# Parking buffers held for good, product banks that swap roles, and earlier splits in the last block

## The chip, the cores and the metric

The kernel runs on one core of one Trainium2 chip. The metric is the device time of one execution in microseconds (us). All tensors are float32, the weights among them arrive as 64-bit floats.

## What is computed

The reference is a chain of three parts: attention within chunks of 64 positions, then two feed-forward layers over 4608 tokens.

```python
scores = (1/8) * q_c @ k_c.T          # 8 batches x 8 heads, chunks of 64, head size 64
attn = softmax(scores); x = (attn @ v_c) -> 4608 x 512
h = x @ w_in          # 512 x 2048
g = max(h, 0) + alpha * min(h, 0)
x = g @ w_out         # 2048 x 512
h = x @ w_in2;  g = h - tanh(h);  out = g @ w_out2
```

(In the code the two layers' weights are moe_w_in, moe_w_out and moe2_w_in, moe2_w_out, or views of them.)

## The kernel before, in words

**Numbers.** TensorE works on pairs: every float32 operand is split into a high part (a rounding copy to fp32r, made by ScalarE) and a low part (operand minus high part, made by VectorE or GpSimd), and each product is three matmuls: high by high, low by high, high by low. Each 64-bit weight block is turned into float32 by two ScalarE instructions (lines 115 and 118) and four VectorE instructions (lines 128, 132, 134, 138), from a raw tile "rw".

**Stages on TensorE.** The tokens are nine blocks of 512. The first two blocks of layer one run in `step_first` and the beginning of the main loop. `step_one` then does layer one for one block by one 128-wide slice of the hidden width per step: 12 matmuls up (line 539), 12 down (line 609, which need the pair "ghi", "glo"), while a table of events (`at(step, fn, place=...)`, fired by `fire` at five places of a step) puts the attention of later blocks, the loads and the weight work between them. From about 742 us on, `two_blocks` runs pairs of blocks with a seven-product scheme (products p1 to p7 of 2x2 blocks, six matmuls each): five passes s = 0 to 4 of eight `cycle(s, p)`, where s = 0 finishes layer one and s = 1 to 4 do layer two; then eight `small(p)` for the last block, and a tail. In a cycle the products go into four banks X, Y (names "hpb") and H0, H1 ("hps"); between them `downs(n)` issues n down matmuls (line 1091) of units in a line, and `split_ahead(n)` makes the pairs of the first n units of that line: "ghi" on ScalarE (line 567), "glo" on GpSimd (line 570). `c11`, `c12`, `c22`, `c21` are the gates that read the finished banks: a few ScalarE instructions (`square`, `second`, `edge`) and VectorE instructions (`drain`, `close`; lines 587, 588, 598 to 600). Line 1190 is the VectorE sum of two banks (`add`), line 1193 the ScalarE copy of a bank.

**Parking.** The seven-product scheme needs sums of weight blocks. They are made in advance and stored ("parked") in device memory. A parking has four functions: `park_load` (DMA of the raw weights into "rw"), `park_form` (conversion and sums), `park_split` (high and low part), `park_store`. There are 16 units of kind "u" (layer two's up weights), each with a unit "u1" (layer one's up weights, which come from pairs already on chip) that goes along with it, one unit in four steps from step 36 on; then 16 of kind "d" (layer two's down weights): six in the last steps of the loop, ten in `two_blocks`, set out there by `when` every 11.5 us of an assumed time. Sums and low parts are made on GpSimd (lines 217, 225, 247), high parts on ScalarE (line 246). Tiles "rw", "mw" and "whi" come from one rotating pool tag with two buffers, "mr" from another with one.

**Order.** The instructions of each engine stay in the order in which the code issues them. All DMAs go through one queue engine, SyncE (SP), in order; a DMA that has to wait for its data holds back those behind it. The queue also carries the loads of queries and keys (line 332), 16 each in a burst, and the fetches of parked weights (line 274).

Of the kernel before, what the change touches and what calls it, by code (L numbers as in the profile page):

```python
# [9 lines left out]
F32 = mybir.dt.float32  # L10
F32R = mybir.dt.float32r
I32 = mybir.dt.int32
U32 = mybir.dt.uint32
I64 = mybir.dt.int64
# [13 lines left out]
def kernel(  # L28
# [19 lines left out]
    nc = tc.nc  # L48
# [3 lines left out]
    P = 128  # L52
# [141 lines left out]
    wu, wd2, parked = {}, {}, {}  # L194

    def park_load(kind, n, c):
        raw = wide.tile([P, 512], I64, tag="w", name="rw")
        if kind == "d":
            load_raw(raw, 1, n, 1)
        else:  # L200
            nc.sync.dma_start(
                out=raw.rearrange("p (g m) -> p g m", g=2),
                in_=w_in2[:, n * 2 * P:(n + 1) * 2 * P].rearrange("(g c p) m -> p g c m", p=P, c=2)[:, :, c, :],
            )
        parked[kind, n, c] = raw

    def park_form(kind, n, c):

        if kind == "u1":
            mr = wide.tile([P, 8, P], F32, tag="w", name="mw")  # L210
# [8 lines left out]
        else:  # L219
            mr = wide.tile([P, 8, P], F32, tag="r", name="mr", bufs=1)  # L220
# [7 lines left out]
    def park_split(kind, n, c):  # L228

        mr = parked[kind, n, c]  # L230
        hi = mr.bitcast(F32R) if kind == "u1" else wide.tile([P, 8, P], F32R, tag="w", name="whi")
# [14 lines left out]
        nc.scalar.activation(out=h, in_=m, func=AF.Copy)  # L246
# [541 lines left out]
    for j in range(2):  # L788
        at(KF + HF * (j + 1) - 1, load_half, j)
    for i in range(KF):  # L790
        n, c, step = i // 2, i % 2, 2 * KF + 4 + 4 * i
        at(step, park_load, "u", n, c)
        at(step, park_form, "u1", n, c)
        at(step + 1, park_split, "u1", n, c)
        at(step + 1, park_form, "u", n, c)
        at(step + 2, park_store, "u1", n, c, place=4)
        at(step + 2, park_split, "u", n, c)
        at(step + 3, park_store, "u", n, c, place=4)
    DP = 6
    for f in range(DP):  # L800
        step = 6 * KF + 4 + 2 * f
        at(step, park_load, "d", f, 0)
        at(step + 1, park_form, "d", f, 0, place=2)
        at(step + 1, park_split, "d", f, 0, place=4)
        at(step + 2, park_store, "d", f, 0, place=1)
# [297 lines left out]
    def split_ahead(n):  # L1103
        for u in line[:n]:
            u.split()
# [36 lines left out]
    def two_blocks(queue):  # L1142
# [6 lines left out]
        H0, H1 = (ps_h.tile([P, NB], F32, tag="h", name="hps") for _ in range(2))  # L1149
        p5 = ptb.rearrange("p e h a i -> p (e h a i)")  # L1150
# [62 lines left out]
        def on(s, p, place, fn, *args):  # L1213
            hooks.setdefault((s, p, place), []).append((fn, args))
# [62 lines left out]
        PLACES = {"start": 0.0, "p1": 1.4, "p5": 2.7, "p6": 4.1, "p2": 5.4, "p3": 6.8, "p7": 8.2, "p4": 12.2, "end": 14.2}  # L1277

        def when(us, fn, *args):
            p, us = divmod(us, 15.0)  # L1280
            place = max((x for x in PLACES if PLACES[x] <= us), key=PLACES.get)
            on(int(p) // NPAIR, int(p) % NPAIR, place, fn, *args)

        todo = []
        for i, f in enumerate(range(DP, KF)):
            todo += [(11.5 * i, park_load, f), (11.5 * i + 5.5, park_form, f), (11.5 * i + 8.5, park_split, f),
                     (11.5 * i + 11.4, park_store, f)]
        for us, fn, f in sorted(todo, key=lambda x: x[0]):
            when(us, fn, "d", f, 0)
        on(1, 0, "start", parks_done)  # L1290

        def cycle(s, p):
            turns = s > 0 and p % 4 == 0
# [65 lines left out]
        def small(p):  # L1359
# [13 lines left out]
            split_ahead(2)  # L1373
# [15 lines left out]
            split_ahead(2)  # L1389
            first.close()  # L1390
            downs(gaps[2])
            product(s, "p4", h1[:, :H], H)
            downs(gaps[3])
# [4 lines left out]
            split_ahead(2)  # L1398
# [61 lines left out]
```

## Time and profile before

| | |
|---|---|
| median of 3 runs | 1739.51 us (1736.46 to 1744.77) |
| the profiled execution | 1742.13 us, span 1740.4 us |
| TensorE matmuls (PE) | 1638.2 us busy, 94% of the span |
| VectorE (DVE) | 1233.6 us, 71% |
| ScalarE (ACT) | 994.7 us, 57% |
| GpSimd (POOL) | 447.5 us, 26% |
| mean granted TensorE clock | 0.975 of full speed |

The profile is of one execution; spans of an engine are its busy times. PE is the engine that is busy nearly all of the time, so the places where it is idle, and those where its clock is granted at less than full speed, are where time can come from. An entry such as "[3.10 <-DVE glo L570]" says that the instruction's engine was idle for 3.10 us before it and that the DVE instruction of line 570, which writes glo, released it.

### The profile page before, as it was taken

Reading aid. Unit: us, or ns where it says so; the run is one execution under the profiler, and the core shown is the slowest. Engines: PE = TensorE matmul, PEld = TensorE weight load, DVE = VectorE, ACT = ScalarE, POOL = GpSimd, SP = SyncE. Lnnn points to the kernel's source line nnn. Section 1 sums busy time; section 2 is a strip of 40 time slices with the busy share of each in tenths; the row PEclk is TensorE's granted clock in tenths of the full one; section 3 lists DMA queues with packets and bytes.
Section 4 is the critical chain, followed back from the end, with each engine's and each line's share of the span. In section 5 each row is a group of like instructions: output and inputs, shape, how many; then the busy total and the mean of one; then the engine's idle time right before and its main releaser. Section 6 shows DMA issues by size and latency. Waiting matters only on the chain.

```text
span 1740.4 us, 26381 instructions
## 1 busy us (share of the span) xinstructions
PE 1638.2 (94%) x9309; PEld 1339.0 (77%) x9309; DVE 1233.6 (71%) x1860; ACT 994.7 (57%) x1785; POOL 447.5 (26%) x406
## 2 busy tenths in 40 slices
PE   7899999989989999998889999999999999999988
PEld 7688887878768787776667877787777778787877
DVE  7878856767767786754367687768776877687763
ACT  5666534555545455554466566656766575656452
POOL 1000002343333342222142223222222232223223
PEclk9999999999999999998989999999999999999999
DMA  9551435556555575366657845554555355535540
GB/s 239 168 184 35 104 89 121 148 159 152 147 127 148 138 183 180 122 215 203 236 188 250 281 147 163 169 173 125 176 157 188 109 176 157 163 110 188 182 132 24
DMA packets 339299, 276.49 MB, mean 159 GB/s; under 512 B 180432, under 2 KB 244960, under 8 KB 339168
## 3 DMA queue, kind: packets, MB, share of 16 engines
q1 hardware_dynamic: 339168, 274.82, 53.4%
q8 instruction: 73, 1.20, 0.3%
q14 instruction: 58, 0.48, 0.1%
HBM read 192.95 MB, written 81.79 MB: 158 GB/s over the span
## 4 chain that ended last, share of the span: by engine, by line
PE 59%; DVE 12%; issue 10%; DMA 5%; ACT 5%; SPq 5%; POOL 4%; DVEq 0%; POOLq 0%; ACTq 0%
PE y L1091 19%; PE hpb L1183 13%; PE hps L539 10%; PE y L609 10%; PE hps L1183 5%; DMA rw<-in_moe_w_out_dram 3%; POOL glo L570 2%; SPq L332 2%; DMA wu<-whi 1%; SPq L298 1%; DVE mr L134 1%; DVE arena L587 1%; DVE mr L128 1%; DVE mr L138 1%; DVE glo L570 1%
## 5 line engine op out<-in xcount | busy, mean ns | idle before, releaser
L539 PE MATMUL hps<-x,w 128*128 128x512 f32 (+1 forms) x1356 | 336.0, 398 | 6.2 <-ACT kt L366 5.3
L570 POOL TENSOR_TENSOR glo<-arena,ghi 128x512 fp32r<-128x512 f32 x142 | 197.1, 1402 | 535.9 <-ACT ghi L567 384.7
L1183 PE MATMUL hpb<-w,wu 128*128 128x512 f32 (+1 forms) x1200 | 296.0, 391 | 28.0 <-DVE th L588 11.7
L539 PEld LDWEIGHTS hps<-x,w 128*128 128x128 f32 x1356 | 260.9, 194 | 62.8 <-ACT kt L366 5.8
L1091 PE MATMUL y<-w,ghi 128*128 128x512 f32 x1152 | 298.7, 392 | 9.7 <-ACT ghi L567 9.7
L1183 PEld LDWEIGHTS hpb<-w,wu 128*128 128x128 f32 x1200 | 226.6, 197 | 79.5 <-DVE th L588 14.2
L1091 PEld LDWEIGHTS y<-w,ghi 128*128 128x128 f32 x1152 | 214.9, 189 | 56.3 <-ACT ghi L567 13.5
L609 PE MATMUL y<-ghi,w 128*128 128x512 f32 x880 | 231.4, 395 | 4.2 <-ACT yst L634 3.5
L609 PEld LDWEIGHTS y<-ghi,w 128*128 128x128 f32 x880 | 161.7, 188 | 40.1 <-ACT yst L634 3.9
L1091 PE MATMUL y<-w,glo 128*128 128x512 f32 x576 | 164.7, 392 | 3.4 <-POOL glo L570 3.4
L1183 PE MATMUL hps<-w,wu 128*128 128x512 f32 (+1 forms) x624 | 138.9, 370 | 13.7 <-DVE hps L1190 13.7
L609 PE MATMUL y<-glo,w 128*128 128x512 f32 x440 | 129.7, 399 | 16.6 <-DVE glo L570 16.6
L1183 PEld LDWEIGHTS hps<-w,wu 128*128 128x128 f32 x624 | 111.0, 191 | 35.8 <-DVE hps L1190 15.4
L1091 PEld LDWEIGHTS y<-w,glo 128*128 128x128 f32 x576 | 108.3, 189 | 28.2 <-POOL glo L570 6.0
L567 ACT ACTIVATE ghi<-g 128x512 fp32r<-128x512 f32 x112 | 70.6, 630 | 95.3 <-DVE g L552 95.0
L552 DVE SCALAR_TENSOR_TENSOR g<-neg,nalpha_sb,g 128x512 f32<-128x512 f32 x112 | 91.8, 820 | 46.2 <-ACT g L551 46.2
L609 PEld LDWEIGHTS y<-glo,w 128*128 128x128 f32 x440 | 83.0, 190 | 37.3 <-DVE glo L570 20.3
L217 POOL TENSOR_TENSOR mw<-w 128x256 f32<-128x256 f32 x32 | 26.9, 860 | 313.8 <-DMA ysc<-yhalf 235.5
L591 ACT ACTIVATE w<-sq,bias_sb 128x512 f32<-128x512 f32 x144 | 104.2, 724 | 0.0
L594 ACT ACTIVATE ktc<-sq,edge_sb 128x512 f32<-128x512 f32 x144 | 103.9, 721 | 0.0
L1193 ACT ACTIVATE hps<-hpb 128x512 f32<-128x512 f32 x40 | 23.3, 582 | 134.4 <-PE hpb L1183 134.4
L599 DVE SCALAR_TENSOR_TENSOR arena<-sq,arena 128x512 f32<-128x512 f32 x116 | 97.0, 836 | 4.0
(171 smaller groups left out, 2562.0 us busy)
## 6 DMA issues: line engine op xcount, KB each, us to landing
wu<-wu SPq DMA_DIRECT2D x336, 256.0 KB, 3.2
g<-arena SPq DMA_DIRECT2D x67, 256.0 KB, 3.6
arena<-g SPq DMA_DIRECT2D x64, 256.0 KB, 3.7
raww<-in_moe_w_in_dram SPq DMA_DIRECT2D x16, 512.0 KB, 5.9
v<-in_v_dram SPq DMA_DIRECT2D x32, 256.0 KB, 3.9
raww<-in_moe_w_out_dram SPq DMA_DIRECT2D x16, 512.0 KB, 5.5
rw<-in_moe_w_in_dram SPq DMA_DIRECT2D x16, 512.0 KB, 5.3
wu<-mw SPq DMA_DIRECT2D x32, 256.0 KB, 3.3
```

The lines of the kernel that those rows point to most:

```text
L217: nc.gpsimd.tensor_tensor(out=quarters[:, :, e], in0=hi, in1=lo, op=ALU.add)
L332: nc.sync.dma_start(out=o, in_=i)
L539: nc.tensor.matmul(out=hp[:, cols], lhsT=w[:, a, m], rhs=x[b][:, kk, cols], start=(kk == 0 and i == 0), stop=(kk == KD - 1 and i == 2),)
L552: nc.vector.scalar_tensor_tensor(out=g, in0=neg, scalar=nalpha_sb[:, f:f + 1], in1=g, op0=ALU.mult, op1=ALU.add)
L567: nc.scalar.activation(out=hi, in_=g, func=AF.Copy)
L570: lo_engine.tensor_tensor(out=lo, in0=g, in1=hi.bitcast(F32), op=ALU.subtract)
L591: nc.scalar.activation(out=self.w, in_=self.sq, func=AF.Square, bias=bias_sb)
L594: nc.scalar.activation(out=self.mask, in_=self.sq, func=AF.Relu, bias=edge_sb)
L599: nc.vector.scalar_tensor_tensor(out=g, in0=self.sq, scalar=TS[0], in1=g, op0=ALU.add, op1=ALU.mult)
L609: nc.tensor.matmul(out=acc[t], lhsT=lhsT, rhs=rhs, start=(f == ends[0] and i == 0), stop=(f == ends[1] and i == 2))
L1091: nc.tensor.matmul(out=self.acc[t], lhsT=lhsT, rhs=rhs, start=(self.f == self.ends[0] and i == 0), stop=(self.f == self.ends[1] and i == 2),)
L1183: nc.tensor.matmul(out=o, lhsT=w[:, a, c], rhs=x[c][:, b, :h], start=start and i == 0 and c == 0, stop=i == 2 and c == 1, skip_group_check ...
```

## The change

- **Desk.** Three fixed tiles are made at step 36: `desk[0]` for raw loads, `desk[1]` for the u1 sums and for all high parts, `desk[2]` for the other sums. The steps of a unit are spread out: load at its first step, u1 sums and split two steps later, the u sums at the third, u split at the fourth, u store at the fifth step. The high part of a u1 unit is made on GpSimd and no longer on ScalarE. The d units are loaded one parking ahead; in `two_blocks` `when` and its times go, and each cycle has one d parking at fixed places (sums at p2, next load at p3, split at p4, store at the end), seven in s = 0 and three in s = 1.
- **Banks.** In odd cycles the pairs (X, Y) and (H0, H1) change places.
- **Last block.** `small` calls `split_ahead(3)` at its start and `split_ahead(2)` after p4, where it called `split_ahead(2)` at its start and after each gate's `drain`.

The line numbers of the kernel after the change are larger by 5 to 13 (park_load 206, park_form 222 and 230, park_split 252 to 255, ghi 575, products 1196, downs 1103).

```diff
--- before.py
+++ after.py
@@ -191,10 +191,15 @@
         {"p6": 0, "p7": 1, "p3": 2, "p5": 3, "p1": 4, "p2": 5, "p4": 6},
         {"p1": 0, "p7": 1, "p2": 2, "p4": 3, "p5": 4, "p6": 5, "p3": 6},
     )
-    wu, wd2, parked = {}, {}, {}
+    wu, wd2, parked, desk = {}, {}, {}, []
+
+    def park_desk():
+        desk.append(wide.tile([P, 512], I64, tag="w", name="rw"))
+        desk.append(wide.tile([P, 8, P], F32, tag="w", name="whi"))
+        desk.append(wide.tile([P, 8, P], F32, tag="r", name="mr", bufs=1))
 
     def park_load(kind, n, c):
-        raw = wide.tile([P, 512], I64, tag="w", name="rw")
+        raw = desk[0]
         if kind == "d":
             load_raw(raw, 1, n, 1)
         else:
@@ -207,7 +212,7 @@
     def park_form(kind, n, c):
 
         if kind == "u1":
-            mr = wide.tile([P, 8, P], F32, tag="w", name="mw")
+            mr = desk[1]
             quarters = mr[:, 0:4].rearrange("p (g e) m -> p g e m", e=2)
             for e in range(2):
                 hi, lo = (
@@ -217,7 +222,7 @@
                 nc.gpsimd.tensor_tensor(out=quarters[:, :, e], in0=hi, in1=lo, op=ALU.add)
             sums = ((3, 1, 3, ALU.add), (1, 0, 1, ALU.subtract), (0, 3, 0, ALU.subtract), (2, 2, 0, ALU.subtract))
         else:
-            mr = wide.tile([P, 8, P], F32, tag="r", name="mr", bufs=1)
+            mr = desk[2]
             flat = mr.rearrange("p s m -> p (s m)")
             to_f32_b([to_f32_a(parked[kind, n, c], flat[:, :512], flat.bitcast(I32)[:, 512:])])
             sums = ((4, 1, 3, ALU.add), (1, 0, 1, ALU.subtract), (5, 4, 0, ALU.subtract), (6, 2, 5, ALU.subtract))
@@ -228,7 +233,7 @@
     def park_split(kind, n, c):
 
         mr = parked[kind, n, c]
-        hi = mr.bitcast(F32R) if kind == "u1" else wide.tile([P, 8, P], F32R, tag="w", name="whi")
+        hi = desk[1].bitcast(F32R)
         if kind == "d":
             wd2[n] = dram.tile([P, 2, 4, P], F32, name=f"wd2_{n}")
             m, h, lo = mr[:, 0:4], hi[:, 0:4], mr[:, 4:8]
@@ -243,7 +248,10 @@
             else:
                 m, h, lo = mr[:, 0:7], hi[:, 0:7], mr[:, 0:7]
                 to = [wu[1, n][:, :, i, c] for i in range(2)]
-        nc.scalar.activation(out=h, in_=m, func=AF.Copy)
+        if kind == "u1":
+            nc.gpsimd.tensor_copy(h, m)
+        else:
+            nc.scalar.activation(out=h, in_=m, func=AF.Copy)
         nc.gpsimd.tensor_tensor(out=lo.bitcast(F32R), in0=m, in1=h.bitcast(F32), op=ALU.subtract)
         parked[kind, n, c] = ((to[0], h.bitcast(F32)), (to[1], lo))
         if kind == "u1" and c == 0:
@@ -787,22 +795,26 @@
         at(s + 1, split_w, d, nc.vector)
     for j in range(2):
         at(KF + HF * (j + 1) - 1, load_half, j)
+    at(2 * KF + 4, park_desk)
     for i in range(KF):
         n, c, step = i // 2, i % 2, 2 * KF + 4 + 4 * i
-        at(step, park_load, "u", n, c)
-        at(step, park_form, "u1", n, c)
-        at(step + 1, park_split, "u1", n, c)
-        at(step + 1, park_form, "u", n, c)
-        at(step + 2, park_store, "u1", n, c, place=4)
-        at(step + 2, park_split, "u", n, c)
-        at(step + 3, park_store, "u", n, c, place=4)
+        at(step, park_load, "u", n, c, place=4)
+        at(step + 2, park_form, "u1", n, c, place=2)
+        at(step + 2, park_split, "u1", n, c, place=2)
+        at(step + 3, park_store, "u1", n, c, place=4)
+        at(step + 3, park_form, "u", n, c)
+        at(step + 4, park_split, "u", n, c)
+        at(step + 5, park_store, "u", n, c, place=2 if i == KF - 1 else 4)
     DP = 6
     for f in range(DP):
-        step = 6 * KF + 4 + 2 * f
-        at(step, park_load, "d", f, 0)
-        at(step + 1, park_form, "d", f, 0, place=2)
-        at(step + 1, park_split, "d", f, 0, place=4)
-        at(step + 2, park_store, "d", f, 0, place=1)
+        step = 6 * KF + 5 + 2 * f
+        if f == 0:
+            at(step - 1, park_load, "d", f, 0, place=4)
+        at(step, park_form, "d", f, 0)
+        at(step + 1, park_split, "d", f, 0)
+        if f + 1 < DP:
+            at(step, lambda f=f: park_load("d", f + 1, 0), place=4)
+            at(step + 2, park_store, "d", f, 0, place=1)
     end = KF * LB
     places = {}
 
@@ -1147,6 +1159,7 @@
         ps_b = ctx.enter_context(tc.tile_pool(name="ps_b", bufs=2, space=bass.MemoryType.PSUM))
         X, Y = (ps_b.tile([P, NB], F32, tag="b", name="hpb") for _ in range(2))
         H0, H1 = (ps_h.tile([P, NB], F32, tag="h", name="hps") for _ in range(2))
+        banks2 = [X, Y, H0, H1]
         p5 = ptb.rearrange("p e h a i -> p (e h a i)")
         arena()
         spare = []
@@ -1274,22 +1287,19 @@
         on(0, 0, "p1", drop, "b11", "b12", "b22", "b21")
         for s in range(NSB + 1):
             border(s)
-        PLACES = {"start": 0.0, "p1": 1.4, "p5": 2.7, "p6": 4.1, "p2": 5.4, "p3": 6.8, "p7": 8.2, "p4": 12.2, "end": 14.2}
-
-        def when(us, fn, *args):
-            p, us = divmod(us, 15.0)
-            place = max((x for x in PLACES if PLACES[x] <= us), key=PLACES.get)
-            on(int(p) // NPAIR, int(p) % NPAIR, place, fn, *args)
-
-        todo = []
+        on(0, 0, "start", park_load, "d", DP, 0)
+        on(0, 0, "p5", park_store, "d", DP - 1, 0)
         for i, f in enumerate(range(DP, KF)):
-            todo += [(11.5 * i, park_load, f), (11.5 * i + 5.5, park_form, f), (11.5 * i + 8.5, park_split, f),
-                     (11.5 * i + 11.4, park_store, f)]
-        for us, fn, f in sorted(todo, key=lambda x: x[0]):
-            when(us, fn, "d", f, 0)
-        on(1, 0, "start", parks_done)
+            s, p = (0, i) if i < 7 else (1, i - 6)
+            on(s, p, "p2", park_form, "d", f, 0)
+            if f + 1 < KF:
+                on(s, p, "p3", park_load, "d", f + 1, 0)
+            on(s, p, "p4", park_split, "d", f, 0)
+            on(s, p, "end", park_store, "d", f, 0)
+        on(1, 4, "start", parks_done)
 
         def cycle(s, p):
+            X, Y, H0, H1 = banks2 if p % 2 == 0 else banks2[2:] + banks2[:2]
             turns = s > 0 and p % 4 == 0
             gaps = (0, 0, 0, 12, 12) if s == 0 else (12, 12, 0, 6, 18) if turns else (0, 0, 0, 12, 36)
             run(s, p, "start")
@@ -1370,7 +1380,7 @@
             run(s, p, "p1")
             while stores:
                 stores.pop(0)()
-            split_ahead(2)
+            split_ahead(3)
             downs(gaps[0])
             product(s, "p6", h1[:, :H], H)
             product(s, "p2", h0[:, :H], H)
@@ -1386,16 +1396,15 @@
             first.second()
             first.edge()
             first.drain()
-            split_ahead(2)
             first.close()
             downs(gaps[2])
             product(s, "p4", h1[:, :H], H)
+            split_ahead(2)
             downs(gaps[3])
             second = gate(s, 1, 2 * p + 1, h1)
             second.square()
             second.second()
             second.drain()
-            split_ahead(2)
 
             def finish():
                 second.edge()
```

On SP, in the middle of the loop of `step_one`, before: the load of a unit's raw weights (rw), the stores of its u1 part (mw and w), a load of values for the attention, the stores of its u part (whi and mr).

```order
113 L201 DMA rw<-in_moe_w_in_dram 128x2x256
114 L258 DMA wu_2_3978<-mw 128x4x128 x2
115 L258 DMA wu_2_3978<-w 128x2x256 x3
116 L293 DMA v<-in_v_dram 128x8x64
117 L258 DMA wu_2_4038<-whi 896x1x128
118 L258 DMA wu_2_4038<-mr 896x1x128
```

After (the u1 part is now in whi too):

```order
112 L206 DMA rw<-in_moe_w_in_dram 128x2x256
113 L266 DMA wu_1_3617<-whi 896x1x128
114 L266 DMA wu_1_3617<-mr 896x1x128
115 L301 DMA v<-in_v_dram 128x8x64
116 L266 DMA wu_2_3970<-whi 128x4x128 x2
117 L266 DMA wu_2_3970<-w 128x2x256 x3
118 L206 DMA rw<-in_moe_w_in_dram 128x2x256
119 L266 DMA wu_2_4141<-whi 896x1x128
120 L266 DMA wu_2_4141<-mr 896x1x128
```

The load of the next unit's raw weights now stands ahead of the u stores of the unit before, with the whole of the next u1 part behind it.

On POOL, one unit in the same loop, before (sums of u1, low part of u1, sums of u, low part of u):

```order
22 L217 TENSOR_TENSOR mw<-w 128x2x128 x2
23 L225 TENSOR_TENSOR mw<-mw 128x128 x4
24 L247 TENSOR_TENSOR mw<-mw 128x512
25 L225 TENSOR_TENSOR mr<-mr 128x128 x4
26 L247 TENSOR_TENSOR mr<-mr,whi 128x896
```

After:

```order
24 L222 TENSOR_TENSOR whi<-w 128x2x128 x2
25 L230 TENSOR_TENSOR whi<-whi 128x128 x4
26 L252 CAST whi<-whi 128x512
27 L255 TENSOR_TENSOR whi<-whi 128x512
28 L230 TENSOR_TENSOR mr<-mr 128x128 x4
29 L255 TENSOR_TENSOR mr<-mr,whi 128x896
```

A CAST of 128x512 (the high part of u1) has come in between, and u1's sums now stand in the tile whi, where the high part of u stands afterwards.

On PE, the beginning of an odd cycle of layer two, before (the last down matmul of the cycle before, then p1, p5 and p6, then p2 and p3, then p7):

```order
2136 L1091 MATMUL y_10343<-w,glo 128x512
2137 L1183 MATMUL hpb<-xo,wu 128x512 x6
2138 L1183 MATMUL hpb<-w,wu 128x512 x12
2139 L1183 MATMUL hps<-w,wu 128x512 x12
2140 L1183 MATMUL hpb<-w,wu 128x512 x6
2141 L1091 MATMUL y_10340<-w,ghi 128x512
```

After:

```order
2136 L1103 MATMUL y_10234<-w,glo 128x512
2137 L1196 MATMUL hps<-xo,wu 128x512 x6
2138 L1196 MATMUL hps<-w,wu 128x512 x12
2139 L1196 MATMUL hpb<-w,wu 128x512 x12
2140 L1196 MATMUL hps<-w,wu 128x512 x6
2141 L1103 MATMUL y_10231<-w,ghi 128x512
```

p1, p5, p6 and p7 now go into the banks named hps, p2 and p3 into those named hpb; order and number are as before.

On ACT, one `small` with its two gates (a gate is lines 582, 583, 591, 594), before:

```order
1552 L1193 ACTIVATE hpb<-hpb 128x256
1553 L1193 ACTIVATE ptb<-hpb 128x256
1554 L594 ACTIVATE ktc<-sq_8794,edge_sb 128x512
1555 L582 ACTIVATE sq_8794<-hpb 128x512
1556 L583 ACTIVATE th<-hpb 128x512
1557 L591 ACTIVATE w<-sq_8794,bias_sb 128x512
1558 L594 ACTIVATE ktc<-sq_8794,edge_sb 128x512
1559 L567 ACTIVATE ghi<-slot 128x512
1560 L582 ACTIVATE sq_8794<-hpb 128x512
1561 L583 ACTIVATE th<-hpb 128x512
1562 L591 ACTIVATE w<-sq_8794,bias_sb 128x512
1563 L567 ACTIVATE ghi<-arena 128x512 x2
```

After (a gate is lines 590, 591, 599, 602):

```order
1531 L1206 ACTIVATE hpb<-hpb 128x256
1532 L1206 ACTIVATE ptb<-hpb 128x256
1533 L602 ACTIVATE ktc<-sq_8650,edge_sb 128x512
1534 L575 ACTIVATE ghi<-arena 128x512 x2
1535 L590 ACTIVATE sq_8650<-hpb 128x512
1536 L591 ACTIVATE th<-hpb 128x512
1537 L599 ACTIVATE w<-sq_8650,bias_sb 128x512
1538 L602 ACTIVATE ktc<-sq_8650,edge_sb 128x512
1539 L575 ACTIVATE ghi<-arena 128x512
1540 L590 ACTIVATE sq_8650<-hpb 128x512
1541 L591 ACTIVATE th<-hpb 128x512
1542 L599 ACTIVATE w<-sq_8650,bias_sb 128x512
```

Two of the three high parts of a `small` (ghi) now stand ahead of the first gate, right behind the copies of p1 and p5; in the rows of before all three stand behind a gate.

## Rows read from the trace of the kernel before

**Rows 1.** Windows, by stage: busy us (instructions) of PE, PEld, DVE, ACT, POOL; granted clock; DMA share.
```profile
255.00:719.00 464.00, 445.31 (x3201) 360.20 (x3200) 336.11 (x536) 241.47 (x457) 167.73 (x200) 0.98 0.57 151
741.70:898.20 156.50, 130.95 (x529) 104.83 (x528) 78.47 (x108) 79.37 (x146) 43.15 (x30) 0.91 0.65 209
898.20:1594.00 695.80, 674.25 (x2935) 553.04 (x2934) 522.05 (x796) 450.69 (x800) 179.24 (x131) 0.99 0.55 172
1594.00:1709.00 115.00, 103.47 (x573) 87.57 (x571) 79.22 (x92) 55.18 (x106) 31.30 (x22) 0.97 0.46 145
```

**Rows 2.** Windows, narrow ones: the same columns.
```profile
287.00:290.40 3.40, 3.40 (x9) 2.62 (x10) 3.40 (x4) 0.64 (x2) 2.10 (x1) 0.50 0.45 135
...
880.90:891.20 10.30, 4.94 (x12) 3.88 (x13) 9.90 (x14) 6.83 (x15) 5.06 (x3) 0.50 0.16 52
...
1345.40:1352.20 6.80, 4.91 (x22) 3.70 (x22) 6.59 (x11) 4.84 (x9) 1.28 (x1) 1.00 0.50 151
1597.70:1604.60 6.90, 6.25 (x19) 5.05 (x19) 4.52 (x5) 2.21 (x4) 2.85 (x3) 0.51 0.37 125
```

**Rows 3.** Timeline, 272 to 290 us: start, us, engine, line, operation, [idle before].
```profile
279.88 0.66 ACT L115 ACTIVATE mr<-rw 128x512 f32<-128x512 f32 x1 [6.68 <-DMA rw<-in_moe_w_in_dram]
...
286.88 1.97 PE L609 MATMUL y<-glo,w 128*128 128x512 f32 x4 [3.10 <-DVE glo L570]
```

**Rows 4.** Waits of PE, 250 to 700 us: us in total, times, longest.
```profile
PE y L609 <- DVE glo L570: 13.2, 6, 3.1
```

**Rows 5.** Timeline of SP's queue, 494 to 513 us.
```profile
496.22 9.26 SPq L332 DMA_DIRECT2D raw<-in_k_dram  x16
505.53 0.45 SPq L201 DMA_DIRECT2D rw<-in_moe_w_in_dram  x1
```

**Rows 6.** Groups by form, 262 to 690 us: busy us, mean ns, idle before and releasers.
```profile
L552 DVE SCALAR_TENSOR_TENSOR g<-neg,nalpha_sb,g 128x512 f32<-128x512 f32 x68 | 59.1, 869 | 24.8 <-ACT g L551 24.8
...
L225 POOL TENSOR_TENSOR mw<-mw 128x128 f32<-128x128 f32 x61 | 35.3, 579 | 4.8
...
L217 POOL TENSOR_TENSOR mw<-w 128x256 f32<-128x256 f32 x30 | 25.5, 868 | 78.4 <-DMA wu<-whi 70.6 <-issue 6.8 <-POOL mr L247 1.0
L247 POOL TENSOR_TENSOR mw<-mw 128x512 fp32r<-128x512 f32 x16 | 21.9, 1371 | 82.6 <-ACT mw L246 73.7 <-DMA raw<-in_q_dram 8.8
```

**Rows 7.** Timeline, 516 to 522 us.
```profile
518.15 2.11 POOL L247 TENSOR_TENSOR mr<-mr,whi 128x896 fp32r<-128x896 f32 x1 [2.35 <-ACT whi L246]
...
518.72 2.09 DVE L552 SCALAR_TENSOR_TENSOR g<-neg,nalpha_sb,g 128x512 f32<-128x512 f32 x1
```

**Rows 8.** Waits of PE, 700 to 930 us.
```profile
PE hps L1183 <- DVE hps L1190: 12.2, 3, 7.3
PE hpb L1183 <- ACT arena L1129: 10.2, 4, 5.0
```

**Rows 9.** Timelines within s = 0, at 848 us and at 872 to 888 us.
```profile
847.95 0.66 ACT L115 ACTIVATE mr<-rw 128x512 f32<-128x512 f32 x1 [7.13 <-DMA rw<-in_moe_w_out_dram]
...
881.13 1.49 DVE L128 TENSOR_SCALAR mr<-mr 128x512 f32<-128x512 f32 x1
...
886.26 2.08 PE L1183 MATMUL hps<-w,wu 128*128 128x512 f32 x4 [7.30 <-DVE hps L1190]
```

**Rows 10.** Waits of PE, 930 to 1600 us.
```profile
PE hpb L1183 <- DVE th L588: 13.7, 7, 2.1
PE hpb L1183 <- ACT th L583: 3.0, 3, 1.0
```

**Rows 11.** Timeline, 1344 to 1358 us: one cycle of layer two.
```profile
1348.85 1.65 PE L1183 MATMUL hpb<-w,wu 128*128 128x512 f32 x6 [1.89 <-DVE th L588]
...
1356.09 1.66 PE L1183 MATMUL hps<-w,wu 128*128 128x512 f32 x6 [1.49 <-DVE hps L1190]
```

**Rows 12.** Waits of PE, from 1594 us to the end.
```profile
PE y L1091 <- ACT ghi L567: 9.7, 10, 2.2
PE y L1091 <- POOL glo L570: 1.9, 3, 0.6
```

## The prediction

> **What bounds the kernel now.** I read the windows by stage first [rows 1]. PE is busy for 445.3 of 464 us in the main loop, 131.0 of 156.5 us in s = 0, 674.3 of 695.8 us in layer two and 103.5 of 115 us in the small cycles. So PE bounds every stage, and the time that can be had is where PE is idle, and where its clock is low. Idle time in these four stages is 18.7 + 25.5 + 21.6 + 11.5 = 77 us. The narrow windows [rows 2] show the clock: behind a long gap PE runs at a granted clock of 0.50, that is 1.2 instead of 2.4 GHz, for some time: 3.4 us at 287 us, 10.3 us at 881 us, 6.9 us at 1597 us. A 3.4 us stretch in which PE is wholly busy at half speed loses half of itself, 1.7 us. So a gap of 3 us costs 4.7 us in all. A gap of 1.89 us at 1349 us [rows 11] did not lower it: its window in rows 2 shows 1.00. Then I read what ended the gaps: the waits of PE by stage, and the timeline around the longest ones.
>
> **Main loop.** The longest gaps look like the one at 287 us [rows 3]. ACT stood idle for 6.68 us at line 115, because the raw weights had not landed; behind it on ACT stand ghi and the copies of the attention, behind these glo on DVE, and PE waits 3.10 us for glo. Such a load is late because SP's queue is held: the one issued at 505.5 us stood behind 9.26 us of key loads [rows 5]. All waits for glo in the loop are 13.2 us, six of them, the longest 3.1 [rows 4]. Not every one has a load in front (one comes from DVE itself, below); I take five sixths, 11 us, and three low-clock stretches of 1.7 us, 5.1 us: 16 us are the loads' doing. The change issues a load three steps before its conversion instead of one, and a step takes some 6.3 us (the 464 us of the stage [rows 1] hold about 73 steps), so a burst of 9 us no longer reaches ACT.
>
> What it adds: 16 CASTs of 128x512 on POOL. The trace of before has no CAST there. From below the nearest row is a 128x128 sum at 0.58 us, from above the low part of the same 128x512 at 1.37 us [rows 6]; I take 1.1 us, nearer to the row of its own size: 16 x 1.1 = 18 us of POOL, which is busy for 168 of 464 us [rows 1] and so has room. ACT loses the same 16 instructions. The cost is indirect: DVE can be held by POOL. At 518 us [rows 7] a DVE instruction of line 552 ran for 2.09 us beside a POOL low part of 2.11 us, where its mean is 0.87 us [rows 6]: 1.2 us more. 16 CASTs can hold DVE 16 times, 20 us at the worst; most of it lies in DVE's idle time (336 of 464 us busy), and I charge one more gap of 1 us with its low-clock stretch, 2.7 us. The Trainium skill speaks against moving this copy: GPSIMD Engine Reference, sections 8 (Key points) and 4.1 (Engine selection), says that GpSimd shares its SBUF interfaces with VectorE and contends with VectorE instructions that have two SBUF inputs, though a one-input operation runs there at about line rate. By the first half of that every CAST beside a DVE sum would cost, and the loop would gain nothing; rows 7 agree for a two-input POOL instruction, and none shows a one-input one. Net for the loop: 16 - 2.7 = 13 us gained, between 0 and 16. The 23 us up to two_blocks I leave as they are.
>
> **s = 0.** PE waits 12.2 us for line 1190's sums and 10.2 us for the gate's second ScalarE instruction [rows 8]. The first are DVE behind the conversion of a d parking: before the 7.30 us gap the first of its four instructions alone ran for 1.49 us, in a cycle that also makes the next pass's operands [rows 9]. The second are ACT held by the raw load, 7.13 us at 848 us [rows 9], with the gate that frees X behind it. The change loads one cycle ahead, puts the conversion behind the sum that p3 needs, leaves the crowded p = 7 without one, and lets the next cycle start in other banks. What is left is PE's own work: 529 matmuls [rows 1] at 674.25 / 2935 = 0.230 us (layer two's mean, at nearly full clock), 121.5 us; plus what remains of p = 7's gap without the conversion, of which I take 3 us, and its low-clock stretch, 1.7. That makes 126.2 us instead of 156.5: 30 us gained. The lower end is half of that, 15 us, if the waits move to p4 (below). Three parkings now lie in layer two, p = 1 to 3 of s = 1, with four DVE instructions each ahead of the sum that p4 or c22 needs. Between nothing and two instructions of 1.49 us each time; I take 1.2 us, 3.5 us lost.
>
> **The bank swap in layer two.** PE waits there at p1, 13.7 us in seven waits for line 588 (the gate's last reading of X) and 3.0 us in three for line 583 [rows 10]. With other banks p1 finds them free. But DVE works off the same queue: in the cycle at 1349 us p1 waited 1.89 us, and p3 still waited another 1.49 us for line 1190's sum [rows 11], which stands behind the closing of two gates. Started earlier, p3 waits longer by up to as much. Upper end: all 16.7 us go. Lower end: every wait only moves to p3, and three more cycles fall to the low clock, 3 x 1.7 = 5 us lost. Rows 11 are nearest, and they show p3 bound by DVE; I take 3 us gained.
>
> **The small cycles.** PE waits 9.7 us for ghi in ten waits and 1.9 us for glo in three [rows 12], and the first of them is followed by 6.9 us at half clock [rows 2], 3.4 us lost: 15.0 us. After the change two of three ghi are issued ahead of the gate that they stood behind, and the third eight matmuls (1.8 us) before its use. ACT is busy for 55 of 115 us [rows 1]; nothing stands in the way. I take 14 us, at least 8.
>
> **Sum.** 13 + 30 - 3.5 + 3 + 14 = 56.5 us. Against the profiled execution, 1742.1, that is 1685.6 us. That execution lies 2.6 us above the median of the three runs (1739.5) and within their spread, so I forecast 1685 us. A measurement of this kernel tells about 0.5% from no change, 8.7 us.
>
> **Rivals.**
> - *The desk chokes the loop* (0.17). desk[1] takes u1's sums, then its high part, then u's high part. POOL's next u1 sums must wait until u's store has landed, and ACT's u copy until u1's has; SP, in order, holds both stores behind bursts of 9 us [rows 5]. For it: POOL already waited 70.6 us for stores of whi [rows 6]. Against: POOL is idle for two thirds of the loop, and the stores have a step each. Then the loop's 13 us don't come: 1698.
> - *The same, on the path: slower* (0.04). If those 70.6 us [rows 6] move from POOL, where they cost nothing, to ACT's copy of u, with ghi behind it, PE waits for them in every unit: 1698 + 70.6 = 1769 us. It decides when u1's store lands more than about a step's slack (6 us) after ACT reaches the copy.
> - *Waits only move in the cycles* (0.18). The conversion now stands ahead of the second sum of line 1190, so that p4's gate comes late, and p3 keeps waiting in layer two: s = 0 gains 15 and the swap loses 5: 1685.6 + 15 + 8 = 1709.
> - *POOL holds DVE* (0.06). Each of the 16 CASTs costs the 1.2 us of rows 6 and 7, on the path: 20 us instead of the 2.7: 1703.
> - *Everything comes* (0.13). The swap gains 9 of its 16.7 us, the CASTs and the three parkings cost nothing: 6 + 2.7 + 3.5 better: 1673.
>
> That the change doesn't do what it says can be left out: the order of the instructions is the one written, as the excerpts show.
>
> **How the numbers follow.** My forecast has 0.42. The cases between 1673 and 1709 hold 0.96; with the bounds of their terms (the small cycles down to 8, s = 0 a few us either way) the range is 1662 to 1712 us, which leaves out the slower case and the ends of the third and the last. All cases but one lie below 1731, the bound of 0.5%: faster 0.94, with 0.02 taken off for a case that falls short of its worth; that is the same 0.02; slower 0.04.
>
> **What would show it.** Right: in the loop no wait of ACT line 115 for rw above 1 us, and PE's waits for glo below 4 us; a window of s = 0 near 126 us; in layer two no wait of p1 for line 588, and some waits of hps or hpb for line 1190 in their stead; no wait for ghi in the small cycles. Wrong: ACT waiting at the u copy for a store of wu, DVE instructions of 2 us beside CASTs, or POOL waiting for stores with ACT behind it; and an s = 0 above 140 us.

## The result, and the profile after

The changed kernel takes 1694.55 us (median of four runs, 1690.63 to 1697.06) against 1740.74 us before (1736.46 to 1744.77): a ratio of 0.973, with a 95% interval from 0.970 to 0.976. It is faster by 46 us. The forecast was 1685 us, 1662 to 1712.

PE's idle time fell, but not everywhere. The two kernels issue the same matmuls, so the starts of the same ones cut both into equal pieces of work: the first p1 of s = 0, of s = 1, of the first small cycle. In windows with these bounds (columns as in [rows 1]) the kernel before has

```profile
255.00:741.70 486.70, 464.63 (x3277) 375.63 (x3277) 353.70 (x560) 254.43 (x481) 173.30 (x204) 0.98 0.55 147
741.70:898.20 156.50, 130.95 (x529) 104.83 (x528) 78.47 (x108) 79.37 (x146) 43.15 (x30) 0.91 0.65 209
898.20:1585.00 686.80, 665.25 (x2881) 545.05 (x2880) 516.48 (x783) 446.09 (x789) 177.00 (x130) 0.99 0.55 171
1585.00:1740.40 155.40, 140.01 (x745) 118.00 (x743) 91.42 (x111) 67.04 (x127) 47.63 (x33) 0.98 0.40 127
```

and the kernel after

```profile
255.00:719.50 464.50, 454.23 (x3270) 370.48 (x3269) 352.59 (x555) 244.52 (x460) 186.96 (x219) 0.99 0.58 154
719.50:847.80 128.30, 122.53 (x529) 100.03 (x528) 66.55 (x97) 74.36 (x138) 37.11 (x28) 0.97 0.72 234
847.80:1555.70 707.90, 672.11 (x2881) 547.03 (x2880) 539.29 (x795) 451.35 (x798) 181.51 (x132) 0.98 0.54 170
1555.70:1693.50 137.80, 133.63 (x745) 116.61 (x743) 78.22 (x111) 67.13 (x127) 46.78 (x33) 1.00 0.45 143
```

So the loop gained 22.2 us, s = 0 28.2 us and the last block with the tail 17.6 us, while layer two became 21.1 us longer: 46.9 in all, the 46.8 us between the two profiled executions (1742.13 and 1695.32). Layer two is the surprise: the same 2881 matmuls, 21 us more.

The waits of PE (us in total, times, longest) show where the old ones went. Of the loop's waits for glo [rows 4] nothing is left in the list; PE waits there now 6.3 us in three for yst (ScalarE, line 642) and once 3.9 us for ktc (VectorE, line 385).

In the small cycles no wait for ghi or glo is left in the list [rows 12]. In layer two 15.7 us in eight waits for VectorE stood before p1 (898 to 1585 us; the window of [rows 10] begins later and has seven of them). Now none is left there, and 27.6 us stand before p3 (whose bank is called hpb in odd cycles), eight of the nine waits 3.3 to 3.5 us long:

```profile
PE hpb L1196 <- DVE hpb L1203: 27.6, 9, 3.5
```

The timeline of one of those cycles (s = 1, p = 5; p1 started at 960.26 us) shows what the added time is made of:

```profile
964.91 2.99 POOL L578 TENSOR_TENSOR glo<-arena,ghi 128x512 fp32r<-128x512 f32 x2 [2.48 <-ACT ghi L575]
965.10 1.67 DVE L607 SCALAR_TENSOR_TENSOR arena<-sq,arena 128x512 f32<-128x512 f32 x1
...
966.88 1.62 DVE L608 COPY_PREDICATED arena<-ktc,th 128x512 f32<-128x512 uint32 x1
...
970.33 2.93 PE L1196 MATMUL hpb<-w,wu 128*128 128x512 f32 x6 [3.47 <-DVE hpb L1203]
```

The two VectorE instructions that close c21 took 1.67 and 1.62 us beside GpSimd's low parts; the same two took 0.69 and 0.77 us a little earlier in this cycle, without it. The clock fell within the gap, and the window from there on is at half clock:

```profile
968.90:975.70 6.80, 5.37 (x13) 4.21 (x14) 2.57 (x5) 2.61 (x5) 0.00 (x0) 0.50 0.19 56
```

That suggests a chain: with p1 and p5 no longer held, their two ScalarE copies and the ghi behind them come earlier, GpSimd's two glo start earlier, and now run beside the closes, which the sum for p3 stands behind. In the kernel before, PE's wait at p1 had kept the two apart. In the same cycle there the last close had ended at 1010.38 us when the low parts began, and in all eight places the two instructions took 0.69 to 0.78 us:

```profile
1009.65 0.73 DVE L600 COPY_PREDICATED arena<-ktc,th 128x512 f32<-128x512 uint32 x1
...
1011.91 2.54 POOL L570 TENSOR_TENSOR glo<-arena,ghi 128x512 fp32r<-128x512 f32 x2 [5.70 <-ACT ghi L567]
```

### The profile page after: what moved, and what is told of

Its sections match the earlier page's. It is cut to its first block, busy times and chain, and to the rows that moved or that the text cites. A ratio compares the mean times of both kernels' runs of the same rounds, so it can differ in the third digit from the quotient of the medians.

```text
span 1693.5 us, 26409 instructions
## 1 busy us (share of the span) xinstructions
PE 1619.7 (96%) x9309; PEld 1329.5 (79%) x9309; DVE 1232.0 (73%) x1860; ACT 986.9 (58%) x1769; POOL 458.8 (27%) x422
## 4 chain that ended last, share of the span: by engine, by line
PE 69%; DVE 13%; ACT 5%; issue 5%; DMA 4%; SPq 3%; POOL 2%; DVEq 0%; ACTq 0%; POOLq 0%
PE y L1103 23%; PE hps L547 12%; PE y L617 12%; PE hpb L1196 10%; PE hps L1196 10%; SPq L340 2%; DVE arena L607 1%; DVE arena L606 1%; DMA ysc<-yst 1%; DVE g L560 1%; DVE arena L608 1%; DMA rw<-in_moe_w_in_dram 1%; DMA wu<-wu 1%; POOL glo L578 1%; DVE arena L595 1%
## 5 line engine op out<-in xcount | busy, mean ns | idle before, releaser
L547 PE MATMUL hps<-x,w 128*128 128x512 f32 (+1 forms) x1356 | 328.4, 392 | 5.9 <-ACT kt L374 5.3
L547 PEld LDWEIGHTS hps<-x,w 128*128 128x128 f32 x1356 | 255.4, 190 | 59.6 <-ACT kt L374 5.8
L1196 PE MATMUL hpb<-w,wu 128*128 128x512 f32 (+1 forms) x912 | 218.3, 383 | 35.7 <-DVE hpb L1203 32.7
L1196 PEld LDWEIGHTS hpb<-w,wu 128*128 128x128 f32 x912 | 165.9, 192 | 73.6 <-DVE hpb L1203 37.2
L1196 PE MATMUL hps<-w,wu 128*128 128x512 f32 (+1 forms) x912 | 215.7, 382 | 3.6 <-ACT hpb L1206 2.1
L1196 PEld LDWEIGHTS hps<-w,wu 128*128 128x128 f32 x912 | 168.0, 194 | 39.9 <-ACT hpb L1206 4.8
L578 DVE TENSOR_TENSOR glo<-g,ghi 128x512 fp32r<-128x512 f32 x111 | 95.9, 864 | 34.9 <-ACT ghi L575 33.8
L222 POOL TENSOR_TENSOR whi<-w 128x256 f32<-128x256 f32 x32 | 26.3, 845 | 333.3 <-DMA ysc<-yhalf 234.0
L558 ACT ACTIVATE neg<-hps 128x512 f32<-128x512 f32 x112 | 66.3, 592 | 76.9 <-PE hps L547 76.7
L608 DVE COPY_PREDICATED arena<-ktc,th 128x512 f32<-128x512 uint32 x118 | 97.9, 830 | 10.2 <-ACT ktc L602 0.6
```

Source lines behind the costliest of these rows:

```text
L547: nc.tensor.matmul(out=hp[:, cols], lhsT=w[:, a, m], rhs=x[b][:, kk, cols], start=(kk == 0 and i == 0), stop=(kk == KD - 1 and i == 2),)
L558: nc.scalar.activation(out=neg, in_=hp, func=AF.Relu, scale=-1.0)
L578: lo_engine.tensor_tensor(out=lo, in0=g, in1=hi.bitcast(F32), op=ALU.subtract)
L608: nc.vector.copy_predicated(g, self.mask.bitcast(U32), self.th)
L1196: nc.tensor.matmul(out=o, lhsT=w[:, a, c], rhs=x[c][:, b, :h], start=start and i == 0 and c == 0, stop=i == 2 and c == 1, skip_group_check ...
```

## The experiments

Twelve kernels ran, each with the kernel before on the same chip. "Layer two" is the time from the first p1 of s = 1 to the first of the small cycles; the columns behind the median are from the one profiled execution (us).

| kernel | median us | s = 0 begins | s = 0 | layer two | last block to last matmul |
|---|---|---|---|---|---|
| before | 1739 to 1741 | 741.7 | 156.5 | 686.8 | 151.5 |
| changed | 1694.6 | 719.5 | 128.3 | 707.9 | 133.6 |
| changed, swap in s = 0 alone | 1678.1 | 720.0 | 128.4 | 687.2 | 133.6 |
| changed, no swap | 1679.9 | 717.1 | 130.6 | 691.2 | 133.6 |
| before, swap alone | 1744.7 | 743.8 | 142.7 | 701.1 | 149.7 |
| before, small cycles alone | 1720.6 | 740.0 | 156.5 | 687.1 | 133.6 |
| changed, split moved in name only | 1697.0 | 721.1 | 128.2 | 709.3 | 133.6 |
| changed, splits behind the gate | 1670.3 | 719.2 | 128.7 | 683.4 | 133.6 |
| ... and c21's close behind the sum | 1660.8 | 717.8 | 128.8 | 674.7 | 133.6 |
| ... and late parkings in s = 1 | 1654.0 | 716.0 | 128.1 | 669.7 | 133.6 |
| ... and splits behind the gate in s = 0, p = 7 | 1657.1 | 718.2 | 132.0 | 671.2 | 133.6 |
| changed, loads one step ahead | 1707.2 | 730.1 | 128.3 | 707.2 | 133.6 |
| changed, u1's high part on ScalarE | 1721.4 | 745.7 | 128.1 | 710.3 | 133.6 |
| changed, both of the last two | 1716.3 | 740.3 | 128.1 | 708.5 | 133.6 |

### Is it the swap?

Swap kept in s = 0 alone:

```diff
-            X, Y, H0, H1 = banks2 if p % 2 == 0 else banks2[2:] + banks2[:2]
+            X, Y, H0, H1 = banks2 if s > 0 or p % 2 == 0 else banks2[2:] + banks2[:2]
```

> The changed kernel with its bank swap kept in s = 0 alone. Theory: in layer two the swap costs. The wait that stood at p1 (1.9 us) moves to p3 and grows to 3.3 to 3.5 us, because the earlier p1 and p5 bring the GpSimd low parts onto the VectorE closes, and the clock stays low longer: about 3 us for each of eight places. Then layer two falls from 707.9 us to 685 to 692 us and the whole to 1673 to 1680 us. Rival: layer two is longer because of the three parkings moved into it and of the queue; then it stays at 700 us or more and the whole at 1688 us or more.

1678.11 us, 0.966 of before (0.963 to 0.968), layer two 687.2 us: as the theory has it, and 16 us better than the changed kernel. The three parkings cannot be the 21 us, since they are still there.

No swap at all (`X, Y, H0, H1 = banks2`):

> The changed kernel with no swap at all. Layer two as in the one with the swap in s = 0 alone (685 to 692 us). Theory: s = 0 needs the swap, p1 there waits again some 1.5 us in each of seven cycles and the clock falls with some of them, so that s = 0 takes 138 to 150 us instead of 128.3 and the whole lies 8 to 20 us above the kernel with the swap in s = 0 alone. Rival: with the raw weights loaded early ScalarE frees X in time, s = 0 stays below 132 us, and the two kernels are alike within 4 us.

1679.86 us, 1.8 us above the one with the swap in s = 0 alone and not clear of it (1678.3 to 1683.5 against 1675.3 to 1681.2), and s = 0 takes 130.6 us: the rival. The swap was put in where PE waited for ScalarE, 10.2 us in four waits [rows 8]; without it, but with the raw weights loaded early, one such wait of 1.7 us is left, so the swap is worth about 2 us there. The layer two of these two kernels is the same code and took 691.2 and 687.2 us: a difference of 4 us between two profiled executions shows nothing by itself.

The swap alone in the kernel before (the two lines on banks2):

> The kernel before with the bank swap alone. Theory: layer two grows from 686.8 us by 12 to 20 us, s = 0 (156.5 us) shrinks by 5 to 12 us, where p1 waited for the gate's ScalarE instruction; the whole is 1740 to 1755 us. Rival: the swap as such gains and its loss in the changed kernel comes from what was changed beside it: layer two 680 us or less, the whole below 1735 us.

1744.68 us, slower by 0.35% (ratio 1.0035, 1.0021 to 1.0049). Layer two grows by 14.3 us, s = 0 shrinks by 13.8 us: the theory, with s = 0 a little better than expected. The swap's two effects are of equal size in the kernel before; in the changed kernel the loss is left and some 2 us of the gain.

### Why does the swap cost?

First try: the splits of the next units written behind the sum of line 1203 in the cycles p = 1 and 5.

```diff
-            split_ahead(2 if turns or s == 0 else 3)
+            if s == 0 or p % 4 != 1:
+                split_ahead(2 if turns or s == 0 else 3)
...
             add(H1, X, p5)
+            if s > 0 and p % 4 == 1:
+                split_ahead(3)
```

> The changed kernel with the swap, but in the cycles p = 1 and 5 of layer two the units' high and low parts are made behind the sum that p3 needs, not ahead of it. Theory: the GpSimd low parts no longer stretch the VectorE closes (1.67 and 1.62 us where they take 0.7 to 0.8 alone), so p3's wait falls from 3.4 to some 1.6 us at eight places; 10 to 20 us less, 1675 to 1685 us. Rival: the closes are late by VectorE's own work; p3's wait stays above 3 us and the time within 4 us of the changed kernel's, 1690 to 1699 us.

1697.00 us, no change, and the timeline is the old one: the closes again 1.67 and 1.62 us, GpSimd at the same place. It decides nothing, since the sum is a VectorE instruction: ScalarE and GpSimd, which make the splits, have the same order as without the edit. What has to be moved is the place on those two engines.

Second try: the splits behind the first gate's ScalarE instructions (`c11.edge()`), under the same condition.

> The changed kernel with the swap, but in the cycles p = 1 and 5 of layer two the high and low parts of the next units are made behind the first gate's ScalarE instructions, so that ScalarE and GpSimd really come to them later (the edit before this one left the order on ScalarE and GpSimd as it was). Theory: GpSimd's low parts no longer run beside the VectorE closes, which fall from 1.6 to 0.7 to 0.8 us each; p3's wait falls from 3.4 to about 1.6 us, layer two from 707.9 to 680 to 695 us, the whole to 1667 to 1682 us. Rival: VectorE's own work holds the sum; p3's wait stays above 2.8 us, layer two above 702 us, the whole above 1689 us.

1670.25 us, layer two 683.4 us. The same cycle now reads:

```profile
962.26 0.69 DVE L607 SCALAR_TENSOR_TENSOR arena<-sq,arena 128x512 f32<-128x512 f32 x1
...
963.05 0.75 DVE L608 COPY_PREDICATED arena<-ktc,th 128x512 f32<-128x512 uint32 x1
...
965.64 1.66 PE L1196 MATMUL hpb<-w,wu 128*128 128x512 f32 x6 [1.61 <-DVE hpb L1203]
```

p3's wait fell from 3.47 to 1.61 us, by as much as the two closes lost (0.98 + 0.87 = 1.85 us), and the clock stays up. So of the 24.5 us that this takes off layer two, eight times 1.85, 15 us, are VectorE beside GpSimd; most of the rest is the clock: it was at half for 27.3 us of the changed kernel's layer two and is at half nowhere in this one's, and PE's busy time there falls from 672.1 to 661.0 us.

With c21's close in these cycles besides put behind the sum:

```diff
-            c21.close()
-            enlist(s, 0, 2 * p + 1, c21.g)
+            def finish():
+                c21.close()
+                enlist(s, 0, 2 * p + 1, c21.g)
+            if turns:
+                later.append(finish)
+            else:
+                finish()
```

(`later` is emptied right behind the next cycle's `add(H1, X, p5)`.)

> As the one with the splits behind the gate, and besides the closing of c21 after a cycle p = 0 or 4 of layer two (three VectorE instructions, some 2.1 us) put behind the sum that the next cycle's p3 needs. Theory: p3's wait falls below 0.8 us at eight places and the clock stays up, layer two takes 665 to 675 us, the whole 1652 to 1663 us. Rival: the work put off holds the next sums, and p4 waits in p3's place; layer two 680 us or more, the whole 1667 us or more.

1660.82 us, layer two 674.7 us, at the edge of what was expected: in p = 1 and 5 no wait for the sum at p3 is left, one of 1.2 us appears at p3 of a cycle p = 6, and in s = 1, p = 1, where a parking's conversion comes on top, p4 waits 2.7 us. Layer two is now 12.5 us shorter than in the kernel with the swap in s = 0 alone. (The close put off without the swap was not tried.)

### The parkings in s = 1, and p = 7

The three parkings in s = 1 converted behind c12's close (place "p7" for "p2", and "end" for "p4"):

> As the one with the splits behind the gate and the closing of c21 behind the sum, and besides the three parkings in s = 1 converted behind c12's close and split at the cycle's end. Theory: their VectorE conversion stood ahead of the sum that p4's gate needs and cost 1.8 us in each of the cycles p = 2 and 3 and more in p = 1; s = 1 falls from 173.4 to 166 to 168 us and the whole to 1652 to 1656 us. Rival: the work then holds the closes at the cycle's end, p1 or p3 of the next cycle waits for it; s = 1 stays above 171 us and the whole above 1658 us.

1653.96 us, the best kernel of the study: 0.952 of before (0.950 to 0.955). s = 1 falls from 173.4 to 168.9 us; not quite to 168, as p = 2 still takes 23.4 us, with a wait of 2.7 us at p3: what the rival foresaw, in one place. The time is not clear of the 1660.82 us without it by the intervals of the two ratios (0.950 to 0.955 and 0.952 to 0.957); the gain is read from s = 1.

The last cycle of s = 0 is the longest there (23.0 us, the others 15.0). In the changed kernel:

```profile
831.31 2.94 POOL L578 TENSOR_TENSOR glo<-arena,ghi 128x512 fp32r<-128x512 f32 x2 [8.00 <-ACT ghi L575]
831.36 3.44 DVE L710 TENSOR_TENSOR arena<-arena 128x512 f32<-128x512 f32 x2
...
835.46 2.93 PE L1196 MATMUL hpb<-w,wu 128*128 128x512 f32 x6 [5.07 <-DVE hpb L1203]
```

The splits of that cycle put behind its first gate too:

> As the one with the splits behind the gate, c21's close behind the sum and the late parkings, and besides the splits of the last cycle of s = 0 (p = 7) behind its first gate. Theory: the 5.1 us wait for the sum of line 1190's kind in that cycle is again VectorE beside GpSimd: two additions took 3.44 us beside the low parts where two take 1.3 us without; with the low parts later the wait falls to some 3 us, the cycle from 23.0 to 19 to 21.5 us, the whole to 1649 to 1652 us. Rival: the operands of the next pass fill VectorE anyway, or the low parts then collide with the next additions; the cycle stays above 22.3 us and the whole at 1652 us or more.

Half right. The two additions take 1.29 us and the wait before p3 is 2.93 us, as expected; but the low parts now run beside the sums of line 700 behind p3 (2.54 us for two, 1.30 in the changed kernel), ghi delays ScalarE's copies ahead of these by another 1.0 us, and the wait before p4 is 3.31 us instead of 0.67 in the changed kernel:

```profile
830.76 1.29 DVE L710 TENSOR_TENSOR arena<-arena 128x512 f32<-128x512 f32 x2
...
835.34 2.54 DVE L700 TENSOR_TENSOR w<-arena,w 128x512 fp32r<-128x512 f32 x2 [1.49 <-ACT w L698]
...
843.12 2.93 PE L1197 MATMUL hps<-w,wu 128*128 128x512 f32 x6 [3.31 <-DVE hps L1204]
```

(The additions that come next stand beside GpSimd in both kernels: 3.48 us in the changed one, 3.45 here.) The cycle takes 26.0 us, the whole 1657.14 us (1653.6 to 1660.9), not clear of the 1653.96 (1652.8 to 1658.4) without it.

### The small cycles

The kernel before with the new `small` alone:

> The kernel before with the last block's part of the change alone (the earlier splits in the eight small cycles). Theory: the waits for ghi and glo go with the low clock behind the first, 151.5 us from the first small cycle to the last matmul become 134 us, as in the changed kernel; the whole is 15 to 20 us shorter than before, 1719 to 1725 us. Rival: part of the 18 us came from a queue or a clock that the other parts left in better shape; then it gains less than 12 us, 1728 us or more.

1720.64 us, 133.6 us from the first small cycle to the last matmul: the theory; the term stands by itself.

### The loop

Loads one step before the conversion (`at(step + 2, park_load, "u", n, c)`):

> The changed kernel with the raw loads of the u units issued one step before their conversion, as in the kernel before, in place of three. Theory: the lead is what the loop gained; ScalarE waits again for rw, PE for glo, s = 0 begins at 731 to 742 us in place of 719.5 and the whole is 11 to 22 us longer, 1706 to 1717 us. Rival: the fixed tiles and the spread of the steps gained it; s = 0 begins within 4 us of 719.5 and the whole stays at 1690 to 1699 us.

1707.18 us, s = 0 begins at 730.1 us: 10.6 of the 22.2 us are given back, just under what the theory had. PE waits less for glo than for the attention's ktc (12.1 us in two waits): there DVE itself had stood for 9.35 us behind a conversion whose raw load was issued behind 31 loads of queries and keys, and the ktc transpose stood behind that. The late load has several victims; which one PE waits for depends on the step.

u1's high part on ScalarE again:

```diff
-        if kind == "u1":
-            nc.gpsimd.tensor_copy(h, m)
-        else:
-            nc.scalar.activation(out=h, in_=m, func=AF.Copy)
+        nc.scalar.activation(out=h, in_=m, func=AF.Copy)
```

> The changed kernel with the 16 high parts of u1 on ScalarE again, no CAST on GpSimd. Theory: the CAST costs nothing and gains something, since it takes ScalarE out of the chain from u1's sums to its store (GpSimd waited 73.7 us for that ScalarE copy before); s = 0 begins 3 to 10 us later than at 719.5 us, the whole is 1697 to 1705 us. Rival: the CASTs beside VectorE cost what was charged for them (2.7 us or more); s = 0 begins 2 us earlier or more, the whole is 1692 us or less.

1721.42 us: the loop gives back 26.2 us, all it had gained and more. The direction is the theory's, the size is far beyond it. The waits of ACT (250 to 700 us) and of PE (250 to 742 us) say why:

```profile
ACT whi L251 <- POOL whi L230: 57.9, 10, 10.6
...
PE hps L544 <- ACT g L556: 13.4, 7, 4.2
```

With one fixed tile for both high parts GpSimd must let the old stores land before it forms the next u1 sums (48.2 us in nine waits in this run), and this schedule splits them in the same step. If ScalarE makes the copy, it waits there, and PE behind it for the bank that g frees. On GpSimd the same wait (45.4 us in the changed kernel) holds nobody. The CAST keeps that wait off ScalarE. The fixed tile alone is not shown to be its cause: with rotating buffers GpSimd waited as well, 70.6 us [rows 6], but the split stood a step behind the sums. A split a step later was not tried with the fixed tiles.

Both at once:

> The changed kernel with the raw loads of the u units one step before their conversion, and the high parts of u1 on ScalarE: of the loop's change only the fixed tiles and the spread of the steps are left. Theory: lead and CAST together are the loop's gain; s = 0 begins at 736 to 744 us (741.7 before) and the whole is 1711 to 1719 us. Rival: the fixed tiles and the spread hold the rest of the gain; s = 0 begins at 728 to 733 us, as with the late loads alone, and the whole is 1703 to 1710 us.

1716.28 us, s = 0 begins at 740.3 us, in the theory's band. But it is no sum: with the CAST gone the loop is no longer with the late loads than with the early ones (740.3 against 745.7). With the ScalarE waits in place the lead shows no gain. In this schedule the loop's gain needs the CAST, and the lead is worth about half of it once the CAST is there; what the fixed tiles do by themselves no run shows.

## Why the prediction was right, and where it was not

Time and direction were right, 1685 us forecast and 1694.55 measured, with one term wrong in sign and two too small in its favour. That the total came within 10 us is in part luck: layer two, forecast at 0.5 us lost (swap and parkings), lost 21.1, and the loop and the last block gained 12.8 us more than forecast, which covered a good half of it.

- **Loop: 13 us forecast, 22.2 measured.** The mechanism (loads late behind q and k, ScalarE, DVE, PE in turn) is the one that came back with the late loads. The size was off in two ways. The 23 us up to two_blocks, left as they were, gained too: two waits for glo, 3.4 us, stood there, and no wait of PE is left. And the CASTs' charge of 2.7 us was not paid. The bounds, 0.58 and 1.37 us, held the price, 0.77 us, and the choice of 1.1 was too high (group by form, 255 to 690 us):

```profile
L252 POOL CAST whi<-whi 128x512 fp32r<-128x512 f32 x16 | 12.3, 772 | 1.0
```

  No VectorE instruction beside a CAST lost more than 0.4 us. The two of line 560 that began while a CAST of 0.61 us ran ended 0.54 us behind it and took 0.93 and 0.94 us, where they take 0.75 alone and 2.09 us in [rows 7]. So the CAST is cheap here because it is short, not because it leaves VectorE alone. The Trainium skill's GPSIMD Engine Reference, section 8 (Key points), ties the contention to VectorE instructions in a 2-port mode or with two SBUF inputs; line 560 has two, and the trace agrees for a one-input GpSimd instruction too.
- **s = 0: 30 us forecast, 28.2 measured.** Seven of eight cycles run at 15 us, PE's own pace; p = 7 kept a wait of 5.07 us, where 3 were assumed, since GpSimd's low parts held DVE.
- **Parkings in s = 1: 3.5 us forecast, 3.6 to 4.5 measured.** In the changed kernel the cycles p = 2 and 3 of s = 1 take 22.2 us where others take 20.4, 3.6 us for both; p = 1 can't be told apart from the swap's loss. Moving them in the better kernel took off 4.5 us (173.4 to 168.9).
- **Bank swap: +3 us forecast, some -20 measured** (707.9 against 687.2 us with the swap in s = 0 alone and 691.2 with none; in the kernel before it lost 14.3). This is the step that failed. "Started earlier, p3 waits longer by up to as much" has the right place and the right engine; the lower end of 5 us lost was too narrow because it took the VectorE queue's length as given. Started earlier, PE also started ScalarE's copies, the splits and GpSimd earlier, and the queue itself grew by 1.85 us at each place, with the clock's loss behind it. The rest of p3's wait, 1.2 to 1.6 us, is the wait that only moved, as forecast: with the low parts out of the way layer two took 683.4 us with the swap, a little under the 687.2 and 691.2 without it. (The splits behind the gate were not run without the swap.) The rows that showed this cost [rows 7] were used for the loop, where it stayed small, and not for the cycles. The cycle taken as the nearest [rows 11] was an exception: its 1.49 us is the only wait for line 1190 that the list for layer two of the kernel before shows, and just there two VectorE sums ahead of it (line 692, at 1353.06 us) took 2.37 us beside the low parts instead of 1.28. Nor was its clock the rule: of the eight waits of 1.9 to 2.1 us at p1, five had half clock behind them.
- **Small cycles: 14 us forecast, 17.9 measured** (151.5 to 133.6): all waits went, the 3.4 us lost at low clock, and besides the small stops before line 570's low parts.

Of the rivals, "waits only move in the cycles" came true for layer two and not for s = 0. "POOL holds DVE" came true in another place than the one named. The desk's wait exists (GpSimd waits 45.4 us for stores of whi, ScalarE 20.1 us), but with the copy on GpSimd it stays off PE's path; the run with the copy on ScalarE shows the rival's chain at work.

## What to carry to other kernels

A wait taken away from PE starts the other engines earlier as well; before pricing it, list what then runs side by side, above all GpSimd's instructions beside a VectorE chain that PE waits for next. To move such work, look at its own engine's order: writing it behind an instruction of another engine moves nothing. And a buffer whose old content has yet to be stored puts that wait on whoever writes it next, and on whoever works behind it: give both to an engine with nobody behind it.

## What was not expected of the hardware

A 128x512 VectorE instruction on data in on-chip memory went from 0.69 to 1.67 us beside a two-input GpSimd instruction, and two additions from 1.29 to 3.44 us. Which of the two began first decided it. In the changed kernel's trace, 29 VectorE instructions of lines 606, 607, 700 and 710 that a GpSimd instruction began beside took 0.67 to 0.69 us, as alone. Of 75 that began while a GpSimd instruction was at work, 69 ended some 0.55 us behind it: 0.80 us with 0.25 us of it left, 1.77 us with 1.22 us left (the other six began inside one that VectorE was itself holding). In the kernel with the swap in s = 0 alone the same two engines meet the other way round, and GpSimd is the one that is held (2.54 us in the kernel before, above):

```profile
964.11 1.30 DVE L700 TENSOR_TENSOR xo<-arena,xo 128x512 fp32r<-128x512 f32 x2
964.17 3.65 POOL L578 TENSOR_TENSOR glo<-arena,ghi 128x512 fp32r<-128x512 f32 x2 [4.16 <-ACT ghi L575]
```

Gaps of 1.2 to 1.6 us in layer two left the granted clock up in the kernel with the splits behind the gate (1.00 in the mean), while at the gaps of 3.3 to 3.5 us in the same places in the changed kernel it fell to 0.50 six times of eight. Gaps of 1.9 to 2.1 us did both: behind five of eight in the kernel before and two of eight in the one with the swap in s = 0 alone it was 0.50.
